# Batch 0 of a linear-attention and MLP kernel: Q cast on its way in the GpSimd queue, narrower weight slices, and a reordered head

## The chip, the core and the metric

The kernel runs on one core of a Trainium2 chip. The metric is the device time of one execution in microseconds (us). Before the change the median of 9 runs is 284.18 us (283.92 to 284.45).

## What is computed

For each of 8 batches and 8 heads (576 rows, 64 columns per head) a K^T V product is formed, Q is multiplied by it, and each row of 64 is divided by its root mean square and scaled by `g_norm`. The heads lie side by side as 4608 rows of 512, and a two-layer MLP with ELU follows.

```python
kv = np.einsum('bhsd,bhse->bhde', k, v)
out = np.einsum('bhsd,bhde->bhse', q, kv)
rms = np.sqrt(np.mean(out * out, axis=-1, keepdims=True) + 1e-06)
x = (out / rms * g_norm).transpose(0, 2, 1, 3).reshape(4608, 512)
h = x @ w_in                                   # 512 -> 2048
g = np.where(h > 0.0, h, np.exp(np.minimum(h, 0.0)) - 1.0)
return g @ w_out                               # 2048 -> 512
```

Inputs and output are fp32; the kernel multiplies in bf16.

## The kernel before, in words

The work is cut into nine groups of 512 rows: group b holds the first 512 rows of batch b, and the ninth holds the last 64 rows of all batches. For each group the attention gives xT (512 features in four blocks of 128, by 512 rows); `mm1` (L446) makes h in eight steps i of two 128-column blocks of w_in each, with four accumulated products a block; `elu` (L474) turns them into gT on ScalarE and VectorE; `mm2` (L507) multiplies pieces of gT by w_out for four row blocks j. The attention of the next group is spread by hand between the products of the current one; the order of the instructions on each engine is the order in which the program is written (`manual_schedule`, L56)[...].

Two kinds of transfers load data. SP's queue (`fetch_q`, L73) moves fp32 as it is. GpSimd's queue casts fp32 to bf16 on the way: `fetch_packed_kv` (L114), `fetch_packed_q` (L96, batches 1 to 7), `load_w_in` (L135), `load_w_out` (L140). [...]

The head, L551 to L755, is batch 0. SP fetches Q of batch 0 in two halves (even and odd heads, 512 KB each). GpSimd issues k and v of batch 0 in eight pieces of two heads, the identity for transposes between them, then w_in in five slices with the edges 0, 512, 768, 1280, 1664 and 2048, then w_out and batch 1. TensorE begins with nine dummy products of zeros (`idle`, L594); more of them stand between the steps, 20 in all. VectorE and ScalarE cast Q to bf16 (`cast_first`, L608), TensorE transposes it in pairs of heads (`turn_first`, L611), and copies put it into qT0.

Batch 0's features come in four columns c (two heads each). For each c: `kv_first` makes K^T V and VectorE copies it to SBUF, `se_first` makes the scores on TensorE, `square_first` squares them on ScalarE, `mean_first` averages them by a product on TensorE, `log_first` and `exp_first` on ScalarE make the inverse root, and `scale_first` on VectorE writes column c of xT. `first(fs, cs)` (L671) then multiplies blocks fs of w_in with columns cs; it makes the first six blocks (24 products) in six banks, and L761 makes the other ten through `mm1` (L465).

From L773 on, the second layer of group 0 is interleaved with the attention of batch 1, in two halves u: `kvu` (K^T V, L357), `seu` (scores), `sq`, `sum`, `inv`, `mulu` (scaling on VectorE), `xu` (transposes and the copy to xT, L404). Group 1's first layer follows at L873. The output of the last group leaves in pieces at L913, the last of them in two halves of 256 columns, each copied by ScalarE (L925) and stored from two queues.

Of the kernel before, what the change touches and what calls it, by code (L numbers as in the profile page):

```python
# [8 lines left out]
FP32 = mybir.dt.float32  # L9
BF16 = mybir.dt.bfloat16  # L10
# [6 lines left out]
def kernel(  # L17
# [20 lines left out]
    J = 4  # L38
# [34 lines left out]
    def fetch_q(b, eng=nc.sync):  # L73

        st = stage_tile("q")[:, 0:2048]
        raw["q", b] = st
        if b < B:
            for s in range(2):
                eng.dma_start(
                    out=st.rearrange("p (s h x) -> p s h x", s=2, h=4)[:, s],  # L80
                    in_=q[b].rearrange("(h s) r d -> s h r d", s=2)[s, :, 0:G, :].rearrange(
                        "h (p j) d -> p h (j d)", j=J
                    ),
                )
# [61 lines left out]
    def copy_on(eng, out_, in_):  # L146
        if eng is nc.scalar:
            nc.scalar.copy(out_, in_)
        else:
            eng.tensor_copy(out=out_, in_=in_)  # L150
# [292 lines left out]

    gT = {}

    def mm1(T, i, cols=(slice(0, 512),), relu=False, home="m1", between=()):  # L446

        if i == 0:
            gT[T] = mlpg.tile([P, FC, G], BF16, name="gT", tag="gT")
        x = xT[T]  # L450
        if home == "m2":
            h_ps = [ps_m2.tile([P, G], FP32, name="h_ps", tag="mm2") for _ in range(2)]
            parts = [(a, a + 1, h_ps[a].rearrange("p (a t) -> p a t", a=1)) for a in range(2)]
        else:
            if home == "at":
                both = at_tile(FP32).rearrange("p (a t) -> p a t", a=2)
            else:
                both = ps_m1.tile([P, 2, G], FP32, name="h_ps", tag="mm1")
            h_ps = [both[:, a, :] for a in range(2)]
            parts = [(0, 2, both)]  # L460
        for cs in cols:
            for a in range(2):
                f = 2 * i + a
                for c in range(KC):
                    nc.tensor.matmul(  # L465
                        h_ps[a][:, cs],
                        lhsT=w_in_sb[:, c, f * P : f * P + P],
                        rhs=x(c, cs),
                        start=(c == 0),
                        stop=(c == KC - 1),  # L470
                    )
        return elu(T, i, parts, relu, between)

    def elu(T, i, parts, relu, between=()):  # L474
# [73 lines left out]

    V, A, Q = nc.vector, nc.scalar, nc.gpsimd

    fetch_q(0)  # L551
    q_raw0 = raw.pop(("q", 0))
    packed_kv(0)
    for c in range(4):
        fetch_packed_kv("k", 0, slice(c, c + 1))
        if c == 2:
            make_identity(nc, ident)
        fetch_packed_kv("v", 0, slice(c, c + 1))
    edges = (0, 512, 768, 1280, 1664, 2048)
    for lo, hi in zip(edges, edges[1:]):  # L560
        load_w_in(slice(lo, hi))
    load_w_out(0, 4)
# [6 lines left out]
    for name in "kv":  # L569
        fetch_packed_kv(name, 1, slice(2, 4))  # L570

    zeros = const.tile([P, 512], BF16, name="zeros")
    nc.vector.memset(zeros, 0.0)  # L573
    means = const.tile([P, P], BF16, name="means")
    nc.vector.memset(means, 0.0)
# [15 lines left out]
    def bank(n):  # L591
        return ps_head.tile([P, G], FP32, name=f"bank{n}", tag=f"bank{n}")

    def idle(ps, n):  # L594
        for _ in range(n):
            nc.tensor.matmul(ps, lhsT=zeros[:, 0:P], rhs=zeros, start=True, stop=True)  # L596

    bank(0), bank(1), bank(2), bank(3)
    kv_ps = ps_head.tile([P, 2, G], FP32, name="kv_ps", tag="kv")
    bank(6), bank(7)  # L600

    idle_ps = bank(1)
    idle(idle_ps, 9)
    q_st = q_raw0.rearrange("p (q h j d) -> p q j h d", q=4, h=2, j=J)
    q_two = attp.tile([P, NPAIR, J, 2, D], BF16, name="q_two", tag="q_two", bufs=1)
    qT0 = attp.tile([P, NPAIR, G], BF16, name="qT", tag="qT")

    def cast_first(pair, eng):  # L608
        copy_on(eng, q_two[:, pair], q_st[:, pair])

    def turn_first(ps, pairs):  # L611
        for r, pair in enumerate(pairs):
            for j in range(J):
                nc.tensor.transpose(ps[:, r, j * P : j * P + P], q_two[:, pair, j], ident)  # L614

    def turned(n):
        return bank(n).bitcast(BF16).rearrange("p (r t) -> p r t", r=2)

    cast_first(0, V)
    cast_first(1, A)  # L620
    qt_ps = turned(3)
    turn_first(qt_ps, (0, 1))
    nc.vector.tensor_copy(out=qT0[:, 0:2], in_=qt_ps)
    idle(idle_ps, 4)
    cast_first(2, V)
    cast_first(3, A)

    kv0 = attp.tile([P, 2, 2, D], BF16, name="kv0", tag="kv0", bufs=1)
    x0 = attp.tile([P, KC, G], BF16, name="xT", tag="xT")
# [22 lines left out]
    def square_first(c):  # L652
        nc.scalar.activation(sq0[c], se0[c], AF.Square)

    def mean_first(c):
        nc.tensor.matmul(mean0[c], lhsT=means, rhs=sq0[c], start=True, stop=True)  # L656
# [22 lines left out]
                    stop=(c == KC - 1),  # L679
                )  # L680

    qt_ps = turned(7)
    turn_first(qt_ps, (2,))
    nc.scalar.copy(qT0[:, 2, :], qt_ps[:, 0, :])
    kv_first(0)
    idle(idle_ps, 1)
    se0[0] = bank(6)
    se_first(0)
    square_first(0)
    qt_ps = turned(0)  # L690
    turn_first(qt_ps, (3,))
    nc.vector.tensor_copy(out=qT0[:, 3, :], in_=qt_ps[:, 0, :])
    idle_ps = bank(3)
    kv_first(1)
    mean0[0] = bank(2)
    mean_first(0)
    log_first(0)
    se0[1] = bank(7)
    se_first(1)
    square_first(1)  # L700
    exp_first(0)
    g_ps = bank(1)
    nc.tensor.matmul(
        g_ps[:, 0:1],
        lhsT=g_row.rearrange("p l d -> p (l d)"),
# [2 lines left out]
        stop=True,  # L708
    )
    nc.vector.tensor_copy(out=g_col, in_=g_ps[:, 0:1])  # L710
    kv_first(2)
    idle(idle_ps, 2)
    se0[2] = bank(1)
    se_first(2)
    square_first(2)
    mean0[1] = bank(0)
    mean_first(1)
    log_first(1)
    exp_first(1)
    idle(idle_ps, 1)  # L720
    kv_first(3)
    scale_first(0)
    idle(idle_ps, 1)
    mean0[2] = bank(2)
    mean_first(2)
    log_first(2)
# [1 line left out]
    se_first(3)  # L728
    square_first(3)
    exp_first(2)  # L730
    idle(bank(0), 2)
    scale_first(1)
    scale_first(2)
    pair = ps_head.tile([P, 2, G], FP32, name="h_ps", tag="kv")
    products = {0: pair[:, 0, :], 1: pair[:, 1, :], 2: bank(6), 3: bank(7), 4: bank(0)}
    first((0, 1, 2, 3), (0,))
    mean0[3] = bank(2)
    mean_first(3)
    log_first(3)
    exp_first(3)  # L740
    scale_first(3)
    products[5] = bank(1)
    first((0, 1, 2, 3), (1, 2))
    first((4,), (0, 1, 2))
    first((0, 1, 2, 3), (3,))
    first((5,), (0, 1, 2))
    first((4, 5), (3,))
    gT[0] = mlpg.tile([P, FC, G], BF16, name="gT", tag="gT")
    single = [
        [(a, a + 1, products[2 * i + a].rearrange("p (a t) -> p a t", a=1)) for a in range(2)]  # L750
# [30 lines left out]
    for j in range(J):  # L781
        mm2_quarter(0, j, 1)
        if j == 1:
            at["kvu0"]()
        if j == 2:
            at["seu0"](scores)
            at["sq0"]()
            at["sum0"]()
    for j in range(J):
        mm2(0, j, 8, 10)  # L790
        if j == 1:
            at["kvu1"]()
            at["inv0"]()
            at["mulu0"]()
    at["seu1"]()
    at["sq1"]()
    at["sum1"]()
    for j in range(J):
        mm2(0, j, 10, 12)
        if j == 1:  # L800
            at["inv1"]()
            at["xu0"](scores[:, 0, :])
# [4 lines left out]
        mm2(0, j, 12, 14)  # L807
    for j in range(J):
        mm2(0, j, 14, FC, hold=j > 1)
        if j == 0:  # L810
            at["xu1"](scores[:, 1, :])
    mm2_out(0, 2)
    mm2_out(0, 3)
# [57 lines left out]
    at, ahead = ahead, attention(3)  # L871
    ahead["qd"]()
    for i in range(8):  # L873
        mm1(1, i, relu=i in (1, 4), home={0: "at", 2: "m2", 5: "m2"}.get(i, "m1"))()
        if i == 3:
            at["kv"]()
    mm2(1, 0, 0, 8)
# [35 lines left out]
    for j, cols in pieces:  # L913
        n = cols.stop - cols.start
        ps = ps_m2.tile([P, DM], FP32, name="o_ps", tag="mm2")[:, 0:n]
        for f in range(FC):
            nc.tensor.matmul(  # L917
                ps,
                lhsT=gT[B][:, f, j * P : j * P + P],
                rhs=w_out_sb[:, f, cols],  # L920
                start=(f == 0),
                stop=(f == FC - 1),
            )
        sb = outp.tile([P, DM], FP32, name="o_last", tag="o_last", bufs=5)[:, 0:n]
        nc.scalar.copy(sb, ps)  # L925
        for l, eng in enumerate((nc.sync, nc.scalar)):
            eng.dma_start(out=rows[l, G:S, j, cols], in_=sb[l * 64 : l * 64 + 64, :])

# [29 lines left out]
```

## Time and profile before

| what | value |
|---|---|
| median of 9 runs | 284.18 us |
| the profiled execution, its own time | 284.04 us |
| its span in the profile | 282.3 us |
| granted TensorE clock | 1.0 |
| TensorE busy | 277.1 us, 98% |
| VectorE / ScalarE / GpSimd busy | 159.3 / 154.5 / 54.7 us |
| GpSimd's transfer queue | 20752 packets, 17.30 MB, 39.9% of 16 engines' span |
| hardware queues of SP and ScalarE | 35348 packets, 17.83 MB, 23.3% |
| GB/s in the first six slices of 7 us | 195, 203, 204, 202, 207, 201 |

The profile covers one execution; times in it count from the start of the span. "Busy" is the time in which an engine executes. The chain of waits is followed back from the last instruction: at each step to what released it, or to the instruction ahead of it on its engine. A line "L674" is line 674 of the kernel above. An issue of a transfer is short; its landing comes later, and "us to landing" is the time between the two.

### The profile page before, as it was taken

How to read it: one execution, taken by the hardware profiler on the slowest of the kernel's cores; microseconds unless marked ns; L12 is line 12 of the kernel's file. 1: busy time of each engine (PE TensorE's matmuls, PEld its weight loads, DVE VectorE, ACT ScalarE, POOL GpSimd, SP SyncE). 2: the span in 40 equal slices, each digit the busy share in tenths (PEclk: the TensorE clock that was granted, in tenths of full speed). 3: DMA queues.
4: the chain of work that ended last, by engine and by line, in shares of the span. 5: the costliest groups of instructions: out<-in, count | busy, mean ns of one | idle time of the engine just before them, and what ended most of it. 6: DMA issues, size and time to landing. Idle time of an engine off the chain costs nothing.

```text
span 282.3 us, 5187 instructions
## 1 busy us (share of the span) xinstructions
PE 277.1 (98%) x2146; PEld 129.7 (46%) x2146; DVE 159.3 (56%) x231; ACT 154.5 (55%) x222; POOL 54.7 (19%) x96
## 2 busy tenths in 40 slices
PE   8999999999999999999999999999999999999994
PEld 3444544445444444444444444444444444444443
DVE  2359353888388546843694469445854585444400
ACT  2779546666487438533863477337823792333311
POOL 7834422251421331006100421012000000000000
PEclk9999999999999999999999999999999999999999
DMA  7999999796992695359835794445333122010122
GB/s 195 203 204 202 207 201 187 197 178 128 190 191 56 157 174 138 74 149 132 188 75 149 94 221 80 116 110 148 58 96 70 78 55 93 0 77 0 74 77 74
DMA packets 56523, 35.99 MB, mean 127 GB/s; under 512 B 32820, under 2 KB 54068, under 8 KB 56500
## 3 DMA queue, kind: packets, MB, share of 16 engines
q0 software_dynamic: 20752, 17.30, 39.9%
q1 hardware_dynamic: 35348, 17.83, 23.3%
q10 hardware_dynamic: 400, 0.52, 0.6%
q8 instruction: 17, 0.28, 0.4%
q14 instruction: 6, 0.05, 0.0%
HBM read 36.70 MB, written 9.44 MB: 163 GB/s over the span
## 4 chain that ended last, share of the span: by engine, by line
PE 98%; DVE 0%; ACT 0%; issue 0%
PE h_ps L465 42%; PE o_ps L512 39%; PE o_ps L917 5%; PE bank L596 2%; PE at L174 2%; PE bank L674 1%; PE at L465 1%; PE at L201 1%; PE h_ps L674 1%; PE bank L614 1%; PE bank L644 1%; PE se_ps L201 1%; PE kv_ps L174 0%; PE at L185 0%; PE se_ps L413 0%; PE bank L656 0%
## 5 line engine op out<-in xcount | busy, mean ns | idle before, releaser
L465 PE MATMUL h_ps<-xT,w_in_sb 128*128 128x512 bf16 x536 | 125.7, 379 | 0.0
L512 PE MATMUL o_ps<-w_out_sb,gT 128*128 128x512 bf16 x512 | 120.5, 379 | 0.0
L477 ACT ACTIVATE elu_e<-h_ps 128x1024 bf16<-128x1024 f32 (+1 forms) x71 | 70.0, 995 | 80.0 <-PE h_ps L465 77.8
L465 PEld LDWEIGHTS <-w_in_sb 128*128 128x128 bf16 x552 | 52.5, 98 | 63.2 <-DVE xT L333 1.7
L512 PEld LDWEIGHTS <-gT 128*128 128x128 bf16 x512 | 49.4, 98 | 58.4 <-DVE gT L496 0.3
L488 DVE TENSOR_SCALAR elu_e<-elu_e 128x1024 bf16<-128x1024 bf16 (+1 forms) x75 | 32.5, 433 | 73.2 <-ACT elu_e L477 73.2
L496 DVE TENSOR_TENSOR gT<-elu_e,h_ps 128x1024 bf16<-128x1024 bf16 (+1 forms) x51 | 60.1, 1179 | 5.7 <-DVE elu_e L488 0.5
L525 ACT COPY o_sb<-o_ps 128x512 f32<-128x512 f32 x32 | 18.6, 586 | 15.4 <-PE o_ps L512 15.4
L218 DVE TENSOR_REDUCE ss<-sq 128x16 f32<-128x1024 bf16 x16 | 19.4, 1218 | 10.8 <-ACT sq L213 10.1
L483 ACT ACTIVATE elu_h<-h_ps 128x1024 bf16<-128x1024 f32 (+1 forms) x20 | 19.5, 990 | 0.0
L150 POOL COPY q_bf<-q_pk 128x512 bf16<-128x512 bf16 x24 | 14.6, 636 | 20.3 <-DMA q_pk<-in_q_dram 20.3
L496 DVE TENSOR_TENSOR gT<-elu_e,elu_h 128x1024 bf16<-128x1024 bf16 x20 | 13.8, 692 | 2.8 <-ACT elu_h L483 1.5
L917 PE MATMUL o_ps<-w_out_sb,gT 128*128 128x512 bf16 (+1 forms) x80 | 14.1, 337 | 0.0
L125 POOL COPY gate<-qT 1x1 bf16<-1x1 bf16 x6 | 1.1, 182 | 63.1 <-DMA qT<-q_bf 63.1
L104 POOL DMA_DIRECT2D q_pk<-in_q_dram x14 | 10.6, 764 | 2.8 <-issue 1.1
L229 DVE TENSOR_TENSOR xs<-at,ss 128x512 bf16<-128x512 f32 x16 | 10.2, 683 | 1.2 <-ACT ss L225 1.2
L917 PEld LDWEIGHTS <-gT 128*128 128x128 bf16 x80 | 7.7, 98 | 6.4 <-DVE gT L496 0.4
L213 ACT ACTIVATE sq<-at 128x1024 bf16<-128x1024 f32 x9 | 9.4, 1043 | 1.6 <-PE at L201 1.0
L118 POOL DMA_DIRECT2D k_pk<-in_k_dram x12 | 8.3, 691 | 4.5 <-DMA w_in_sb<-in_moe_w_in_dram 3.0
L118 POOL DMA_DIRECT2D v_pk<-in_v_dram x12 | 8.3, 688 | 4.4 <-DMA w_out_sb<-in_moe_w_out_dram 1.8
L596 PE MATMUL bank<-zeros 128*128 128x512 bf16 x20 | 7.8, 518 | 1.2 <-DVE zeros L573 1.2
L925 ACT COPY o_last<-o_ps 128x512 f32<-128x512 f32 (+1 forms) x5 | 2.5, 501 | 10.8 <-PE o_ps L917 10.8
(79 smaller groups left out, 139.5 us busy)
## 6 DMA issues: line engine op xcount, KB each, us to landing
out_dram<-o_sb SPq DMA_DIRECT2D x16, 512.0 KB, 3.1
q_pk<-in_q_dram POOLq DMA_DIRECT2D x14, 256.0 KB, 4.8
k_pk<-in_k_dram POOLq DMA_DIRECT2D x6, 576.0 KB, 7.6
v_pk<-in_v_dram POOLq DMA_DIRECT2D x6, 576.0 KB, 10.6
st_q<-in_q_dram SPq DMA_DIRECT2D x2, 512.0 KB, 5.6
w_in_sb<-in_moe_w_in_dram POOLq DMA_DIRECT2D x2, 512.0 KB, 8.9
w_out_sb<-in_moe_w_out_dram POOLq DMA_DIRECT2D x2, 512.0 KB, 15.6
w_out_sb<-in_moe_w_out_dram POOLq DMA_DIRECT2D x4, 256.0 KB, 11.8
```

The lines of the kernel that those rows point to most:

```text
L118: nc.gpsimd.dma_start(out=raw[name, b].rearrange("p h j d -> p h (j d)")[:, hs], in_=in_[:, hs])
L150: eng.tensor_copy(out=out_, in_=in_)
L218: nc.vector.reduce_sum(out=ss, in_=sq.rearrange("p c (h e) -> p (c h) e", h=H), axis=AX.X)
L465: nc.tensor.matmul(h_ps[a][:, cs], lhsT=w_in_sb[:, c, f * P : f * P + P], rhs=x(c, cs), start=(c == 0), stop=(c == KC - 1),)
L477: nc.scalar.activation(e[:, lo:hi, :], ps, AF.Exp)
L483: nc.scalar.activation(h[:, lo:hi, :], ps, AF.Relu)
L488: nc.vector.tensor_scalar(out=e[:, lo:hi, :], in0=e[:, lo:hi, :], scalar1=1.0, scalar2=1.0, op0=ALU.min, op1=ALU.subtract,)
L496: nc.vector.tensor_tensor(out=gT[T][:, 2 * i + lo : 2 * i + hi, :], in0=e[:, lo:hi, :], in1=h, op=ALU.add if relu else ALU.max,)
L512: nc.tensor.matmul(o_ps[T, j], lhsT=gT[T][:, f, j * P : j * P + P], rhs=w_out_sb[:, f, :], start=(f == 0), stop=(f == FC - 1),)
L525: nc.scalar.copy(o_sb[T][:, j % 2, :], o_ps.pop((T, j)))
L596: nc.tensor.matmul(ps, lhsT=zeros[:, 0:P], rhs=zeros, start=True, stop=True)
L917: nc.tensor.matmul(ps, lhsT=gT[B][:, f, j * P : j * P + P], rhs=w_out_sb[:, f, cols], start=(f == 0), stop=(f == FC - 1),)
```

## The change

In batch 0's head, Q no longer comes through SP. It is fetched by the GpSimd queue, cast on the way, in two halves of four heads (256 KB each in bf16): heads 0 to 3 ahead of all other transfers, heads 4 to 7 behind the second v piece. The casts on VectorE and ScalarE go. Each half is transposed by 16 transposes of 64-column heads (`turn_heads`, eight of 128 columns before) and copied by one VectorE instruction. The first 1280 columns of w_in come in five slices of 256 (before: 512, 256, 512). The steps of the four columns are reordered: the product for `g_norm` comes earlier, heads 4 to 7 are transposed behind the second K^T V, the second mean comes ahead of the third scores. The dummies are cut from 20 to five, two of them in fp32, for which the tile of zeros is doubled. `first` makes blocks 0 and 1 for columns 0 and 1 ahead of blocks 2 and 3.

In batch 1, the second K^T V stands behind all four pieces (8, 10) of the second layer and not behind the second of them; its scores, squares and sums stand behind the first piece (10, 12), and its transposes behind the third piece (14, FC). The first step of group 1's first layer goes through both blocks column by column (`by_c`). In the last store the ScalarE copy of 256 columns becomes two of 128, one on VectorE.

Of the waits in TensorE's list: the first transpose waits for heads 0 to 3, the transposes of heads 4 to 7 stand ahead of the first mean product, blocks 2 and 3 of `first` wait for the second slice of w_in, block 4 for the third.

```diff
-    def mm1(T, i, cols=(slice(0, 512),), relu=False, home="m1", between=()):
+    def mm1(T, i, cols=(slice(0, 512),), relu=False, home="m1", between=(), by_c=False):
...
-            for a in range(2):
+            steps = [(a, c) for a in range(2) for c in range(KC)]
+            if by_c:
+                steps.sort(key=lambda step: step[1])
+            for a, c in steps:
                 f = 2 * i + a
...
-    fetch_q(0)
-    q_raw0 = raw.pop(("q", 0))
+    q_first = packed.tile([P, H, J, D], BF16, name="q_pk", tag="q")
+
+    def fetch_heads(eng, out_, lo):
+        eng.dma_start(
+            out=out_.rearrange("p (h x) -> p h x", h=4),
+            in_=q[0, lo : lo + 4, 0:G, :].rearrange("h (p j) d -> p h (j d)", j=J),
+        )
+
+    fetch_heads(nc.gpsimd, q_first[:, 0:4].rearrange("p h j d -> p (h j d)"), 0)
     packed_kv(0)
     for c in range(4):
         fetch_packed_kv("k", 0, slice(c, c + 1))
-        if c == 2:
+        fetch_packed_kv("v", 0, slice(c, c + 1))
+        if c == 1:
             make_identity(nc, ident)
-        fetch_packed_kv("v", 0, slice(c, c + 1))
-    edges = (0, 512, 768, 1280, 1664, 2048)
+            fetch_heads(nc.gpsimd, q_first[:, 4:8].rearrange("p h j d -> p (h j d)"), 4)
+    edges = (0, 256, 512, 768, 1024, 1280, 1664, 2048)
...
-    zeros = const.tile([P, 512], BF16, name="zeros")
+    zeros = const.tile([P, 1024], BF16, name="zeros")
...
-    def idle(ps, n):
+    def idle(ps, n, dtype=BF16):
+        z = zeros.bitcast(dtype)
         for _ in range(n):
-            nc.tensor.matmul(ps, lhsT=zeros[:, 0:P], rhs=zeros, start=True, stop=True)
+            nc.tensor.matmul(ps, lhsT=z[:, 0:P], rhs=z[:, 0:512], start=True, stop=True)
...
-    idle(idle_ps, 9)
+    idle(idle_ps, 2, FP32)
+    idle(idle_ps, 1)
...
+    def turn_heads(u):
+        qt_ps = turned(3)
+        for s in range(2):
+            for j in range(J):
+                for l in range(2):
+                    nc.tensor.transpose(
+                        qt_ps[l * 64 : l * 64 + 64, s, j * P : j * P + P],
+                        q_first[:, 4 * u + 2 * l + s, j, :],
+                        ident,
+                    )
+        nc.vector.tensor_copy(out=qT_u[:, u], in_=qt_ps)
+
+    turn_heads(0)
...
     kv_first(0)
...
+    idle(idle_ps, 1)
+    se0[0] = bank(6)
+    se_first(0)
+    square_first(0)
+    kv_first(1)
+    turn_heads(1)
+    mean0[0] = bank(2)
+    mean_first(0)
+    log_first(0)
+    se0[1] = bank(7)
+    se_first(1)
+    square_first(1)
+    exp_first(0)
     kv_first(2)
-    idle(idle_ps, 2)
+    mean0[1] = bank(0)
+    mean_first(1)
+    log_first(1)
+    idle(idle_ps, 1)
     se0[2] = bank(1)
     se_first(2)
     square_first(2)
...
-    first((0, 1, 2, 3), (0,))
+    first((0, 1), (0, 1))
     mean0[3] = bank(2)
     mean_first(3)
...
-    first((0, 1, 2, 3), (1, 2))
+    first((2, 3), (0, 1))
+    first((0, 1, 2, 3), (2,))
     first((4,), (0, 1, 2))
-    first((0, 1, 2, 3), (3,))
-    first((5,), (0, 1, 2))
-    first((4, 5), (3,))
+    first((0, 1, 2, 3, 4), (3,))
+    first((5,), range(KC))
...
     for j in range(J):
         mm2(0, j, 8, 10)
-        if j == 1:
-            at["kvu1"]()
...
+    at["kvu1"]()
     for j in range(J):
         mm2(0, j, 10, 12)
+        if j == 0:
+            at["seu1"]()
+            at["sq1"]()
+            at["sum1"]()
...
         mm2(0, j, 14, FC, hold=j > 1)
-        if j == 0:
+        if j == 2:
             at["xu1"](scores[:, 1, :])
...
-        nc.scalar.copy(sb, ps)
+        if cols.stop == DM and n < DM:
+            nc.scalar.copy(sb[:, 0 : n // 2], ps[:, 0 : n // 2])
+            nc.vector.tensor_copy(out=sb[:, n // 2 : n], in_=ps[:, n // 2 : n])
+        else:
+            nc.scalar.copy(sb, ps)
```

More of the change, by code (lines that the diff above doesn't have):

```diff
@@ L461, in mm1 @@
         for cs in cols:
-            for a in range(2):
+            steps = [(a, c) for a in range(2) for c in range(KC)]
+            if by_c:
+                steps.sort(key=lambda step: step[1])
+            for a, c in steps:
                 f = 2 * i + a
[L464 to L471, printed above, removed]
+                nc.tensor.matmul(
+                    h_ps[a][:, cs],
+                    lhsT=w_in_sb[:, c, f * P : f * P + P],
+                    rhs=x(c, cs),
+                    start=(c == 0),
+                    stop=(c == KC - 1),
+                )
         return elu(T, i, parts, relu, between)
@@ L602 @@
     idle_ps = bank(1)
-    idle(idle_ps, 9)
-    q_st = q_raw0.rearrange("p (q h j d) -> p q j h d", q=4, h=2, j=J)
-    q_two = attp.tile([P, NPAIR, J, 2, D], BF16, name="q_two", tag="q_two", bufs=1)
+    idle(idle_ps, 2, FP32)
+    idle(idle_ps, 1)
     qT0 = attp.tile([P, NPAIR, G], BF16, name="qT", tag="qT")
[L608 to L614, printed above, removed]
     def turned(n):
         return bank(n).bitcast(BF16).rearrange("p (r t) -> p r t", r=2)
[L619 to L626, printed above, removed]
+    qT_u = qT0.rearrange("p (s u) t -> p u s t", u=2)
+    def turn_heads(u):
[7 more added lines that the diff above has]
+                        ident,
+                    )
+        nc.vector.tensor_copy(out=qT_u[:, u], in_=qt_ps)
+    turn_heads(0)
     kv0 = attp.tile([P, 2, 2, D], BF16, name="kv0", tag="kv0", bufs=1)
@@ L680, in first @@
                 )
-    qt_ps = turned(7)
-    turn_first(qt_ps, (2,))
-    nc.scalar.copy(qT0[:, 2, :], qt_ps[:, 0, :])
     kv_first(0)
[L686 to L702, printed above, removed]
+    g_ps = bank(2)
     nc.tensor.matmul(
@@ L715 @@
     square_first(2)
-    mean0[1] = bank(0)
-    mean_first(1)
-    log_first(1)
     exp_first(1)
-    idle(idle_ps, 1)
+    scale_first(0)
     kv_first(3)
-    scale_first(0)
-    idle(idle_ps, 1)
     mean0[2] = bank(2)
@@ L730 @@
     exp_first(2)
-    idle(bank(0), 2)
     scale_first(1)
@@ L734 @@
     pair = ps_head.tile([P, 2, G], FP32, name="h_ps", tag="kv")
-    products = {0: pair[:, 0, :], 1: pair[:, 1, :], 2: bank(6), 3: bank(7), 4: bank(0)}
-    first((0, 1, 2, 3), (0,))
+    products = {0: pair[:, 0, :], 1: pair[:, 1, :], 2: bank(6), 3: bank(0), 4: bank(7)}
+    first((0, 1), (0, 1))
     mean0[3] = bank(2)
@@ L788 @@
             at["sum0"]()
+    at["inv0"]()
+    at["mulu0"]()
     for j in range(J):
         mm2(0, j, 8, 10)
-        if j == 1:
-            at["kvu1"]()
[L793 to L797, printed above, removed]
+    at["kvu1"]()
     for j in range(J):
         mm2(0, j, 10, 12)
+        if j == 0:
+            at["seu1"]()
+            at["sq1"]()
+            at["sum1"]()
         if j == 1:
@@ L873 @@
     for i in range(8):
-        mm1(1, i, relu=i in (1, 4), home={0: "at", 2: "m2", 5: "m2"}.get(i, "m1"))()
+        mm1(1, i, relu=i in (1, 4), home={0: "at", 2: "m2", 5: "m2"}.get(i, "m1"), by_c=i == 0)()
         if i == 3:
```

## The prediction

> **What bounds the kernel now.** I read the page first (busy shares), then the chain of work that ended last in order of time, then the timeline and the transfers of the first 20 us.
>
> ```profile
> PE 277.1 (98%) x2146; PEld 129.7 (46%) x2146; DVE 159.3 (56%) x231; ACT 154.5 (55%) x222; POOL 54.7 (19%) x96
> ```
>
> TensorE is busy in all but 5.2 us of the 282.3 us span. 1.2 of these lie ahead of its first instruction and 3.9 behind its last (the last copy and store). So the end is "when TensorE starts real work, plus that work, plus the tail". The chain, whose columns are start, length, engine and line, shows which of its work is padding:
>
> ```profile
> 1.22 4.02 PE bank L596 x9
> 5.24 0.85 PE bank L614 x8
> ...
> 13.89 0.54 PE bank L596 x2
> 14.43 0.49 PE h_ps L674 x2
> ...
> 18.48 1.51 PE bank L674 x7
> 20.00 5.18 PE h_ps L465 x24
> ```
>
> L596 are dummy products. From 14.43 on all is needed: the 24 head products of L674 and one mean product end at 20.00, and from there no wait is left in the chain. What started the products is in the timeline:
>
> ```profile
> 14.32 0.55 PEld L674 LDWEIGHTS <-w_in_sb 128*128 128x128 bf16 x4 [0.38 <-DMA w_in_sb<-in_moe_w_in_dram]
> 15.58 0.75 DVE L665 SCALAR_TENSOR_TENSOR xT<-bank,g_col,r 128x512 bf16<-128x512 f32 x1 [0.78 <-ACT r L662]
> 17.00 0.75 DVE L665 SCALAR_TENSOR_TENSOR xT<-bank,g_col,r 128x512 bf16<-128x512 f32 x1 [0.67 <-ACT r L662]
> ```
>
> The first weight slice ended the wait (issued 7.05, 7.2 us to landing); the xT columns arrive just in time behind it. So the head is bound by transfers. For the first 20 us, in 40 slices of 0.5 us, and for the first k issue (1.24) and five later Q issues of 256 KB that found the GpSimd queue empty (each answer for a stretch with that issue alone):
>
> ```profile
> GB/s 0 0 0 8 31 211 385 383 381 384 273 246 222 196 212 198 203 207 203 196 210 203 198 207 211 205 207 192 227 186 198 203 207 213 205 194 204 208 201 198
> k_pk<-in_k_dram POOLq DMA_DIRECT2D x1, 144.0 KB, 5.5
> ```
> ```profile
> q_pk<-in_q_dram POOLq DMA_DIRECT2D x1, 256.0 KB, 4.1
> q_pk<-in_q_dram POOLq DMA_DIRECT2D x1, 256.0 KB, 4.2
> q_pk<-in_q_dram POOLq DMA_DIRECT2D x1, 256.0 KB, 4.3
> q_pk<-in_q_dram POOLq DMA_DIRECT2D x1, 256.0 KB, 4.4
> ```
>
> Q of batch 0 moves at 384 GB/s on SP's queue as fp32 (1 MB) up to 5 us; from then on the GpSimd queue, which casts, moves 200 GB/s of bf16. Its first packet is at 4.95, 3.7 us after the issue.
>
> [...] 1.46 to 1.58 us in the five later starts, 3.7 at the head. [...] beside a 16 KB instruction packet at 14.3 one engine falls 1.0 us behind (15 parts of the second w_in slice by 15.62, the last at 16.70), and stays so in all later slices. [...] dummies start 0.427 us apart up to 6.3 and 0.22 from 6.74 on.
>
> **The change part by part.**
> *Queue.* SP loses 1 MB; the GpSimd queue gains 2 x 256 KB, heads 0-3 ahead of everything, heads 4-7 behind the second v slice. Moving them costs about the same (1 MB at 384 is 2.7 us; 512 KB in 512-byte packets at 1.37 us each, the distance of the two Q landings in the later starts, is 2.74). What matters is when heads 0-3 land; I call that q0. Lower: 4.35 (packets at 2.7 as in the later starts, full rate at once: 1.24 + 1.46 + 1.37 + 0.25 spread). Upper: 6.5 (first packet at 4.95 as now). I take 1.24 + 4.3 = 5.5, the middle of five starts of the same transfer.
> *Slices behind it.* Eight k/v slices land 0.71 apart (7 steps from 6.77 to 11.74): 5.68. Heads 4-7 and the first two w_in slices of 256 columns: 3 x 1.37 = 4.11. I add 0.2 for switching between Q and k (in the later starts k took 0.2 to 0.7 more than 576 KB at 205), and the 1.0 lag, because the instruction packet came just as the w_in wait opened, at PE row 240, which the changed order has at the same place. The second slice lands at q0 + 11.0 = 16.5; now the first 512 columns have landed at 14.28.
> *Products.* Four products and the mean need only the first slice (about 14.1) and the xT columns 0 and 1; 25 less these is 20 products x 0.216 = 4.32 behind the second slice: end at q0 + 15.3 = 20.8, against 20.0. Break-even: q0 = 4.7.
> *Head chain.* The two casts before transposes go (0.43 DVE, 0.62 ACT), as do 17 of 20 bf16 dummies; of five products left two are fp32. All lay under transfers: nothing. The 16 transposes of heads 4-7 stand ahead of the first mean product, so behind their wait are that product, the log on ACT and all 11 ACT steps behind it. Heads 4-7 land at 5.5 + 0.2 + 2.84 + 1.37 = 9.9, transposes 0.5 (32 took 1.01 at L185), mean 0.22: log at 10.7 against 10.06. The chain's last exp ends at 17.6 (now 16.96), its xT column at 18.3, 9 products later 20.3: hidden behind 20.8.
> *zeros* doubles: memset 0.27 to 0.55, dummies from 1.5: hidden. g's product earlier: hidden.
> *Batch 1.* The queue is about 1.4 later by the end of w_in (5.5 + 0.2 + 5.68 + 1.37 + 5 x 1.37 + 2 x 1.95 + 1.0 = 24.5, now 23.06), TensorE 0.8 later: waits lose 0.6 of slack. First k/v half: landed 33.63, used 34.93: 0.7 stays. Second: 37.81 against 38.48, and moved behind four more products (0.86): 0.9 stays. w_out columns 10-12: 39.06 against 40.20, scores moved behind them (0.34): 0.2 stays. Nothing is paid; if that cover goes, 0.2 to 0.5. The transposes moved to j == 2 come at 45.4 in today's times, their xs at 44.9; x at 46.7, while by_c gives the first group of batch 1 four products (to 47.3) that don't need it: nothing.
> *Tail.* The last copy, 0.37 on ACT, is halved over two engines: 0.0 to 0.2 gained, I take 0.1.
> Sum: +0.8 - 0.1 = +0.7 on the profiled execution's own 284.04 (span 282.3 and 1.7 around it) is 284.7; the median lies 0.14 above that execution: 284.9.
>
> **Rivals.**
> 1. *Late start* (q0 6.5): the 3.7 us at the head belong to the queue's first use and not to SP's traffic. For: packets start at once at full share at 4.95, with none of the slow ramp of the later starts. Against: SP held the engines at 384 GB/s just until then. End at 21.8: +1.7, 285.9.
> 2. *Early start*, the other side: SP's 1 MB was all that held the GpSimd queue back; with it gone heads 0-3 land at 4.35. Price: q0 + 15.3 = 19.65, or with no switching loss 19.45: -0.35 to -0.55, the tail 0.1; without the instruction lag on the second slice, another 0.3 until the ACT chain binds. 283.3 to 283.7. It decides below q0 = 4.6. Against: all five later starts took 4.1 to 4.4 in an otherwise nearly quiet DMA.
> 3. *Nothing to see*: q0 about 5.0 (in the later starts landing came 1.9 us after the third issue ended, which is at 3.1 here), or the instruction packet elsewhere (-1.0 from the second slice, then the ACT chain holds 20.3). End at 20.0 to 20.3: 284.1 to 284.5.
> 4. *Cold clock*: [...] nothing fills 5.4 to 7. If the clock then rises a window later, scores, means and transposes double along the chain: about +1.5, 286.4.
>
> **How the numbers follow.** Main case 0.37 (284.6 to 285.3), late start 0.20, cold clock 0.05, nothing to see 0.22, early start 0.16. A measurement of this kernel can tell about 0.2% (0.57 us) from no change: faster is the early start, 0.16; within 0.2% are rival 3 and a small part of the main case, 0.25; slower 0.59. The range leaves out half of the early start and the worst of the slow ones: 283.5 to 286.0; the main case alone has 284.6 to 285.3.
>
> **What would show it.** In the profile after: the first Q wait of TensorE ends near 5.5; the second w_in slice near 16.5 ends a TensorE wait of about 1 us inside L683; L467 starts near 20.8 and no wait follows. Wrong if Q lands before 4.7, if that wait is absent, or if dummies and scores keep 0.427 spacing past 7.

## The result and the profile after

| what | before | after |
|---|---|---|
| median | 284.18 us | 288.71 us (10 runs, 286.65 to 290.03) |
| after against before | | 1.0159, interval 1.0146 to 1.0173 |
| the profiled execution, its span | 284.04, 282.3 | 288.75, 287.0 |
| heads 0 to 3 of Q landed | (SP, in halves by pairs) | 5.96 |
| heads 4 to 7 of Q landed | | 10.76 |
| first logarithm on ScalarE | 10.06 | 12.44 |
| first product with w_in, L683 | 14.32 | 17.14 |
| product 25, the first of L467 | 19.83 | 24.46 |
| last product ends | 278.44 | 283.01 |

The change makes the kernel 1.6% slower, and the prediction (284.9) was wrong by 3.8 us. The loss is in the head: 4.63 of the 4.7 us that the span grew are there at product 25 (24.46 less 19.83), and behind it TensorE has no gap. TensorE's busy share does not show it (97% against 98%), since a product at half clock counts as busy too (four take 1.71 us on the chain below, where five take 1.08 at full clock). From the page of after:

```profile
PE 279.8 (97%) x2149; PEld 131.8 (46%) x2149; DVE 159.5 (56%) x230; ACT 152.7 (53%) x219; POOL 58.0 (20%) x100
```

The chain of waits of after for the first 26 us (start, length, engine and line):

```profile
4.81 5.95 DMA q_pk<-in_q_dram
...
10.80 1.06 PE bank L628 x16
11.87 0.55 PE bank L665
...
12.44 0.69 ACT r L668
...
17.20 1.82 PE h_ps L683 x4
19.02 0.43 PE bank L665
19.45 1.71 PE bank L683 x4
21.16 0.44 PE h_ps L683 x2
21.60 1.08 PE bank L683 x5
22.68 0.43 PE h_ps L683 x2
23.11 1.51 PE bank L683 x7
```

Two things are to be seen. The chain now enters through the landing of heads 4 to 7 (L628 are their transposes, L665 is the mean, L668 the logarithm). And four products take 1.82 and 1.71 where later five take 1.08: 0.43 to 0.46 each against 0.216. Up to 21 us TensorE runs at half clock. The timeline of TensorE in after tells the same from the start on (start, length, line, operation, count, and in brackets the idle time ahead with what ended it):

```profile
1.49 4.21 PE L607 MATMUL bank<-zeros 128*128 128x512 f32 x5 [1.49 <-DVE zeros L583]
6.01 1.07 PE L628 MATMUL bank<-ident,q_pk 128*64 128x128 bf16 x16 [0.31 <-DMA q_pk<-in_q_dram]
7.84 0.69 PE L174 MATMUL kv_ps<-v_pk,k_pk 64*64 64x64 bf16 x18 [0.77 <-DMA v_pk<-in_v_dram]
10.80 1.06 PE L628 MATMUL bank<-ident,q_pk 128*64 128x128 bf16 x16 [0.18 <-DMA q_pk<-in_q_dram]
17.14 1.89 PE L683 MATMUL h_ps<-xT,w_in_sb 128*128 128x512 bf16 x4
```

The two fp32 dummies are four records, 0.853 us apart behind the first, and with the bf16 one they end at 5.69. Then come a wait, transposes, another wait: nothing dense any more. In the trace's record of the granted clock, before goes to full at 6.74 and stays; in after the first entry, to full, is at 21.06. (The view by stretches prints 1.00 ahead of a first entry, so there the spacing has to be read.) The mean clock shown for the other nine runs of after is 0.976 to 0.987: 0.982 means 0.018 x 287 / 0.5 = 10.3 us at half clock. Half clock ahead of a first entry is not in such a mean (the profiled run is shown with 1.0), so these nine had a recorded stretch at half, most likely as in experiment 3 below, where the clock rose, fell and rose again and the mean is 0.976; no trace of them was kept. Their times follow it: 286.65 at 0.987, 288.07 to 288.71 at 0.981 and 0.982, 289.51 to 290.03 at 0.976.

The transfers of after, GB/s in 40 slices of the first 20 us:

```profile
GB/s 0 0 0 0 1 12 51 147 140 200 195 155 141 166 189 199 178 193 189 215 194 198 201 196 201 192 190 184 199 198 193 196 222 183 192 193 199 195 198 207
```

Packets of the GpSimd queue now begin at 2.84 and not at 4.95, but from 3 to 6 us they move only 148 GB/s on average. The tail, from the timeline of after:

```profile
283.05 0.27 ACT L926 COPY o_last<-o_ps 128x128 f32<-128x128 f32 x1 [1.37 <-PE o_ps L917]
283.35 0.29 DVE L927 COPY o_last<-o_ps 128x128 f32<-128x128 f32 x1 [11.40 <-ACT o_last L926]
```

VectorE's half of the last copy waits for ScalarE's half: 0.59 from first start to last end, where the undivided copy takes 0.37.

### The profile page after: what moved, and what is told of

Read it like the earlier page. It is cut to its first block, busy times and chain, and to the rows that moved or that the text cites. A ratio compares the mean times of both kernels' runs of the same rounds, so it can differ in the third digit from the quotient of the medians.

```text
span 287.0 us, 5189 instructions
## 1 busy us (share of the span) xinstructions
PE 279.8 (97%) x2149; PEld 131.8 (46%) x2149; DVE 159.5 (56%) x230; ACT 152.7 (53%) x219; POOL 58.0 (20%) x100
## 4 chain that ended last, share of the span: by engine, by line
PE 94%; DMA 2%; POOL 1%; ACT 1%; issue 0%; DVE 0%; POOLq 0%
PE h_ps L467 41%; PE o_ps L514 39%; PE o_ps L917 5%; DMA q_pk<-in_q_dram 2%; PE at L174 2%; PE bank L683 1%; PE at L467 1%; PE at L201 1%; PE h_ps L683 1%; PE bank L665 1%; PE se_ps L201 0%; PE bank L653 0%; ACT sq L662 0%; POOL k_pk L118 0%; PE bank L628 0%
## 5 line engine op out<-in xcount | busy, mean ns | idle before, releaser
L467 PE MATMUL h_ps<-xT,w_in_sb 128*128 128x512 bf16 x536 | 125.7, 379 | 0.0
L467 PEld LDWEIGHTS <-w_in_sb 128*128 128x128 bf16 x552 | 52.5, 98 | 63.2 <-DVE xT L333 1.7
L218 DVE TENSOR_REDUCE ss<-sq 128x16 f32<-128x1024 bf16 x16 | 19.4, 1218 | 11.0 <-ACT sq L213 10.3
L174 PEld LDWEIGHTS <-k_pk 64*64 64x64 bf16 x576 | 7.8, 112 | 4.8 <-issue 4.7
L224 ACT ACTIVATE ss<-ss,eps_col 128x16 f32<-128x16 f32 x16 | 5.1, 317 | 4.1 <-DVE ss L218 4.1
```

The costliest lines, as they stand in the source:

```text
L174: nc.tensor.matmul(kv_ps[l * 64 : l * 64 + 64, s, u * 64 : u * 64 + 64], lhsT=bf["k", T][rows, j, 2 * u + l, :], rhs=bf["v", T][rows, j, 2 ...
L218: nc.vector.reduce_sum(out=ss, in_=sq.rearrange("p c (h e) -> p (c h) e", h=H), axis=AX.X)
L467: nc.tensor.matmul(h_ps[a][:, cs], lhsT=w_in_sb[:, c, f * P : f * P + P], rhs=x(c, cs), start=(c == 0), stop=(c == KC - 1),)
```

## The experiments

The theory after the result: the removed dummies had kept the clock up, and without them the clock stays or falls back to half (the gap form). A rival inside it: the clock is late because the dummies are fp32 (the fp32 form). A rival beside it: the later landing of Q and the new order of the head hold the chain, whatever the clock does. The kernel before, run beside each of them, had medians of 283.97 to 284.08.

### 1. The kernel before with fp32 dummies

```diff
-    idle(idle_ps, 9)
+    idle(idle_ps, 2, FP32)
+    idle(idle_ps, 1)
```

> The kernel before with one edit: the first nine bf16 dummies become two fp32 and one bf16 (as in the changed kernel); the four dummies at 5.9 us and all other work stay. Clock theory, fp32 form (fp32 products do not count towards the rise of the clock): the clock rises one or two windows later than 6.7 us, products stand 0.427 us apart until then, 285.5 to 287.5 us. Clock theory, gap form (what is missing are dummies between 5.4 and 8 us): they are still here, so 6.7 us and 284.2. Queue theory (the later landing of Q and w_in made the time): nothing of the queue is changed, 284.2.

Measured: 284.46 (283.97 to 285.59), 1.0018 [1.0004, 1.0032]. The clock rose at 5.92 and stayed, product 25 started at 19.91, 0.08 later than in before. The fp32 form, which asked for 285.5 or more, falls. Four of the 12 runs took 285.12 to 285.59; the trace kept is of one at 284.19 and doesn't tell why.

### 2. The kernel before with its later dummies thinned out

Nine of the eleven dummies behind the first nine are gone, nothing else.

```diff
-    idle(idle_ps, 4)
...
-    idle(idle_ps, 2)
+    idle(idle_ps, 1)
...
-    idle(idle_ps, 1)
...
-    idle(idle_ps, 1)
...
-    idle(bank(0), 2)
```

> The kernel before with nine of the eleven later dummies taken out; the first nine bf16 ones and one ahead of the first and of the third scores stay. Clock theory, gap form: the clock rises late, 285.5 to 287.5 us. Fp32 form: the nine are bf16, the clock rises at 6.7 us as now, 284.1 to 284.3. Queue theory: 284.2.

Measured: 287.86 (287.01 to 288.88), 1.0139 [1.0107, 1.0170]. The view by stretches of this kernel (stretch and its length, busy time and count for PE, PEld, DVE, ACT and POOL, then the granted clock, DMA share, GB/s):

```profile
5.00:7.00 2.00, 1.00 (x9) 0.76 (x8) 0.97 (x3) 0.47 (x2) 1.20 (x3) 1.00 1.19 233
7.00:9.00 2.00, 1.74 (x29) 1.04 (x29) 0.44 (x2) 1.05 (x3) 1.86 (x3) 1.00 1.21 203
9.00:11.00 2.00, 2.00 (x26) 0.99 (x23) 0.72 (x2) 1.18 (x3) 2.00 (x4) 0.54 1.21 203
...
17.00:19.00 2.00, 2.00 (x6) 0.76 (x5) 0.35 (x1) 1.15 (x2) 0.70 (x1) 0.50 1.29 204
19.00:21.00 2.00, 2.00 (x10) 0.84 (x9) 0.75 (x1) 0.16 (x1) 0.71 (x1) 0.90 1.31 203
```

The clock is full after the nine first dummies (from 5.76), falls to half at 9.17 and is full again at 19.41. The 3.41 us ahead of the fall hold one long wait (1.22), where four dummies had stood. From the timeline of the same kernel:

```profile
7.21 0.40 PE L614 MATMUL bank<-ident,q_two 128*128 128x128 bf16 x4 [1.22 <-DVE q_two L150]
```

Only dummies were taken out. The slices of w_in land 0.1 to 0.5 later than in before, but no product waits for them, and yet product 25 starts at 22.80 in place of 19.83. Dummies that the prediction held for covered by transfers were worth 3.8 us. The gap form is shown, in the kernel before. (The two slowest of the four runs are shown with a mean clock of 1.0, like the profiled run of after: that figure alone doesn't tell that the clock was held.)

### 3. The kernel after with bf16 dummies ahead

```diff
-    idle(idle_ps, 2, FP32)
+    idle(idle_ps, 8)
```

> The changed kernel with its two fp32 dummies replaced by eight bf16 ones of the same length in total (3.4 us); all else stays. Fp32 form of the clock theory: the clock rises by 7 to 10 us, the first layer starts near 21.3 us, 285.2 to 286 us. Gap form: the clock stays at half until about 21 us, 288.7. Queue theory: 288 to 288.7.

Measured: 288.96 (288.42 to 289.78), 1.0168 [1.0143, 1.0192]. The clock rose at 5.73, fell at 9.15, rose at 22.80. As in 2, dense dummies at the start are not enough: behind the gaps at 5.5 (0.52) and 6.7 (1.14) the clock goes down again, and the one at 10.0 (1.18) lies behind the fall. The time is that of the gap form, but the course is not: it had the clock at half throughout.

### 4. The kernel after with some gaps filled

```diff
-    idle(idle_ps, 2, FP32)
-    idle(idle_ps, 1)
+    idle(idle_ps, 10)
...
     turn_heads(0)
+    idle(idle_ps, 2)
...
+    idle(idle_ps, 1)
     turn_heads(1)
```

> The changed kernel with ten bf16 dummies first, two more behind the transposes of heads 0 to 3 and one more ahead of those of heads 4 to 7, all in places where TensorE waits for a transfer. Clock theory, both forms: the clock rises near 7 us, products stand 0.216 us apart, the first layer's second part starts near 21.3 us; of the 4.5 us that the change costs 1.2 to 1.5 stay (the queue's share): 285.2 to 285.7 us. Queue theory: 288 to 288.7.

Measured: 287.16 (285.87 to 288.55), 1.0103 [1.0055, 1.0151]: between the two forecasts. It falls into two groups: two runs whose mean clock is 0.997 and 1.0 took 285.87 and 286.06, two with 0.987 and 0.988 took 288.27 and 288.55. In the profile, one of the latter, the clock fell at 13.57, behind a wait of 1.40 us for heads 4 to 7. The same kernel with the clock held and with it lost for a time is thus 2.4 us apart.

### 5. The kernel after with the clock held

Ten dummies ahead, and 4, 1, 6, 3, 3 and 2 at the later places.

```diff
     turn_heads(0)
+    idle(idle_ps, 4)
...
     square_first(0)
     kv_first(1)
+    idle(idle_ps, 6)
     turn_heads(1)
...
     exp_first(0)
+    idle(idle_ps, 3)
```

> The changed kernel with bf16 dummies in every place where TensorE waits in the head (10, 4, 1, 6, 3, 1, 3 and 2 of them)[...]. If the clock's falling back is most of the change's cost: it rises near 6 us and stays, products stand 0.216 us apart, and what remains over the kernel before is the queue's share: 285.4 to 286.0 us, runs within 0.5 us of each other. If the clock is only a small part and the later Q is the main one: 287 us or more even with a held clock.

Measured: 286.71 (286.65 to 286.91), 1.0098 [1.0083, 1.0113]: between the two forecasts. In the profile the clock rose at 6.45 and stayed, and the four runs lie within 0.3 of each other. Product 25 starts at 22.15, still 2.3 later than in before. From the chain of this kernel:

```profile
10.01 1.40 PE bank L607 x6
11.41 0.57 PE bank L627 x16
11.98 0.32 PE bank L665
12.30 0.33 PE bank L653 x2
12.63 0.75 PE bank L607 x3
```

The transposes (L627) take 0.57 and not 1.06, but the dummies (L607) now lie on the chain: the landing of heads 4 to 7 at 11.16 was over when the six ended. Each one too many costs its 0.216.

### 6, 7 and 8. Three attempts at what is left

In 6, heads 0 to 3 came by SP in fp32 and were cast on VectorE and ScalarE, heads 4 to 7 stayed in the GpSimd queue. In 7, all of Q came by SP, and the GpSimd transfer of heads 4 to 7 went. In 8 (kernel 5 otherwise), the transposes of heads 4 to 7 stood behind the first mean and the second scores. All three had dummies at much the same places as kernel 5, in 6 and 7 fewer of them.

```diff
-    fetch_heads(nc.gpsimd, q_first[:, 0:4].rearrange("p h j d -> p (h j d)"), 0)
+    q_st = stage_tile("q")
+    sp_heads(q_st[:, 0:1024], 0)
+    sp_heads(q_st[:, 1024:2048], 4)
...
-            fetch_heads(nc.gpsimd, q_first[:, 4:8].rearrange("p h j d -> p (h j d)"), 4)
```

The diff is that of 7; 6 has neither its last added nor its last removed line.

> As x5, but heads 0 to 3 come by SP as fp32 (512 KB) and are cast on VectorE and ScalarE; heads 4 to 7 stay in the GpSimd queue. If the queue's first 4.5 us are what is left of the cost: heads 0 to 3 ready by 5.1 instead of 6.0, all GpSimd transfers about 1 us earlier than in x5, head end near 19 to 19.7: 283.0 to 283.8 us. If the order of the head (transposes of heads 4 to 7 ahead of the first mean, narrow slices) is what is left: 285 us or more.

Measured: 286.07 (285.42 to 286.16), 1.0066 [1.0050, 1.0083]. The first forecast was missed; the time is in the range of the second, but the chain names a landing and not the order. Heads 0 to 3 landed at 4.46, but heads 4 to 7 only at 11.02, because one of the 16 DMA engines brought its part 1.3 us behind the others (9.73); the first mean came at 11.64. The wait for the second half of Q sets the chain, not that for the first.

> As x5, but all of Q comes by SP as fp32 in two transfers of four heads and is cast on VectorE and ScalarE, as in the kernel before; slices, order and tail are those of the changed kernel. Queue theory of the rest: the second w_in slice lands near 14.5 to 15.5, head end 19 to 20: 283.0 to 284.0 us. If slices and order are what is left: 285 us or more.

Measured: 287.36 (285.93 to 288.97), 1.0121 [1.0073, 1.0168]. Inconclusive: TensorE waited 1.49 us for v at 6.69, and the clock fell at 8.93. The two runs with a mean clock of 0.999 and 1.0 took 286.39 and 285.93.

> As x5, but the transposes of heads 4 to 7 stand behind the first mean product and the second scores, so that ScalarE's chain no longer waits for heads 4 to 7 (10.8 us). If that wait sets the head's end (through the 11 ScalarE steps behind it): log at about 10.2 instead of 11.8, head end 0.5 to 1 us earlier than x5. If the second w_in slice sets it (at q0 + 15.3): as x5 within 0.2 us.

Measured: 286.88 (286.34 to 288.53), 1.0112 [1.0081, 1.0144], as 5. The clock held. The first logarithm came at 10.62 (in 5 at 12.34), but product 25 at 22.32. The dummies that fill the moved place are on the chain in its stead, so this run doesn't tell what the place of the transposes is worth.

### 9 and 10. Clock held with fewer dummies, and Q on SP beside it

9 is kernel 5 with 10, 4, 4, 1, 2 and 1 dummies. 10 is kernel 7 with 8, 6, 2, 1, 3 and 1; six of them fill the wait for v.

> The changed kernel with bf16 dummies only where they should end ahead of the awaited transfer (10, 4, 0, 4, 1, 1, 2 and 1), nine fewer in the middle than a full fill puts on the chain. With the clock held, the head ends at 21.2 to 21.8 us (x5: 22.4), 285.5 to 286.0 us: what the queue and the order cost with a full clock. If the dummies of x5 were not on the chain: 286.6 as x5. If the fill is too thin the clock falls back: 287 us or more, runs spread over more than 1 us.

Measured: 286.43 (285.79 to 287.48), 1.0083 [1.0068, 1.0098]; product 25 at 21.51, as expected, the time 0.4 above its forecast. Against after the held clock is worth 288.71 - 286.43 = 2.3 us, net of what its dummies cost on the chain. At product 25 it is 2.95; some is given back at 41.45, where TensorE waits 0.32 for a slice of w_out.

> The changed kernel with all of Q on SP in fp32 and cast on VectorE and ScalarE, and dummies set for these arrivals (8, 6, 2, 0, 1, 1, 3 and 1), so that the clock holds where x7 lost it. If the GpSimd transfer of Q is what is left of the cost with a full clock: the first mean no longer waits for heads 4 to 7, head end near 20, 283.8 to 284.5 us. If the order and the slices are what is left: 285.5 us or more.

Measured: 285.46 (285.27 to 286.00), 1.0052 [1.0040, 1.0064]; clock full from 6.22, product 25 at 20.74. So Q in the GpSimd queue costs 286.43 - 285.46 = 1.0 us, with dummies set for each of the two; how much of it is the dummies' was not run apart. The time lies at the edge of the forecast by which order and slices are left. From the chain of 10:

```profile
9.86 0.40 PE kv_ps L174 x18
10.26 0.57 PE bank L642 x16
10.83 0.34 PE bank L682
```

Q has long landed (6.85), and still the first mean (L682) comes at 10.83, behind the 16 transposes (L642).

### 11 to 14. The other parts, in the kernel before

11 takes over the moves in batch 1, `by_c` and the split of the last copy; 12 the narrow slices of w_in and the new order of the 24 products; 13 the split of the last copy alone; 14 is 11 without it. Their diffs are the parts of the change's diff.

> The kernel before with only the late parts of the change: batch 1's second K^T V, its scores and its transposes later, the first step of group 1 column by column, and the last copy halved over ScalarE and VectorE. The head is untouched. By the prediction batch 1's moves cost and gain nothing and the tail gains 0.1. By the profile of the changed kernel the two halves run one after the other (0.27 and 0.29 us), so the tail loses 0.1 to 0.2: 284.1 to 284.3 us. Over 284.5 us: the moves cost something that no wait showed.

Measured: 284.54 (284.36 to 284.93), 1.0018 [1.0011, 1.0025]: more than expected. Product 25 at 19.82 and the last product's end at 278.37 are unmoved.

> The kernel before with only the narrow w_in slices and the new order of the first 24 products; Q, dummies and head chain as before. The first slice lands at about 13.1, but xT's first column is there at 14.1 and the last dummies end at 14.4: the products start where they did, and the second slice is there by 15.4: 283.8 to 284.3 us. If narrow slices by themselves cost transfers or waits: 284.7 us or more.

Measured: 284.05 (283.93 to 284.80), 1.0003 [0.9995, 1.0011]. The first slices landed at 13.07 and 14.40; the products start at 14.22 as before.

> The kernel before with the last store's copy split over ScalarE and VectorE, nothing else. If the tail is the whole of the +0.5 that tail and batch-1 moves cost together: 284.4 to 284.6, with TensorE's last end unmoved at 278.4 and the second half of the copy starting where the first ends. If only the later end of the copy counts (0.56 in place of 0.37): 284.2 to 284.3.

Measured: 284.61 (284.41 to 284.98), 1.0021 [1.0013, 1.0029]: the split copy is the whole of it, +0.57. From the end of the last product to the end of the span it is 4.29 us (282.8 less 278.51) where it was 3.86. The stores are issued 0.22 later behind that product (0.66 in place of 0.44), and the rest is their landing, some 0.2 longer. From the timeline of 13:

```profile
278.55 0.27 ACT L926 COPY o_last<-o_ps 128x128 f32<-128x128 f32 x1 [1.37 <-PE o_ps L917]
278.85 0.29 DVE L927 COPY o_last<-o_ps 128x128 f32<-128x128 f32 x1 [11.40 <-ACT o_last L926]
```

> The kernel before with the moves in batch 1 and the column-by-column step of group 1, the tail as it was. If these cost nothing, as the prediction had it: 283.9 to 284.2. If they take part in the +0.5: 284.3 to 284.5, with a gap of TensorE between 38 and 50 us.

Measured: 283.99 (283.82 to 284.06), 0.9997 [0.9989, 1.0006]: the moves in batch 1 cost nothing.

### 15. Q on SP, clock held, transposes early

```diff
     cast_heads(q_st[:, 1024:2048], 4)
-    idle(idle_ps, 6)
+    idle(idle_ps, 5)
+    turn_heads(1)
...
-    idle(idle_ps, 2)
+    idle(idle_ps, 1)
     kv_first(1)
-    turn_heads(1)
```

> The kernel after with all Q on SP and the clock held by bf16 dummies (the version at 285.46), and the transposes of heads 4 to 7 directly behind those of heads 0 to 3, five dummies between them, ahead of the wait on the first v piece; one dummy less ahead of the second K^T V. If the place of these transposes is most of what is left of the loss: first mean at about 10.2 (before 10.06, there 10.8), end of the 24 products at 20.0 to 20.4, 284.7 to 285.1. If the transfers or the dummies of the later head hold it: no change, 285.3 to 285.6. The clock has to be full from about 6.5 on for either to be read.

Measured: 285.11 (284.94 to 285.61), 1.0038 [1.0026, 1.0051]; product 25 at 20.49, 0.25 ahead of 10. The transposes of heads 4 to 7 also have a bank of their own here. Just outside the weak end of what the order theory expected: in this profile the mean came at 10.56, behind a copy of qT (0.69) that the scores wait for.

### 16. The last copy in two tiles

```diff
-        nc.scalar.copy(sb, ps)
+        if cols.stop == DM and n < DM:
+            for a, copy in enumerate((nc.scalar.copy, nc.vector.tensor_copy)):
+                sb = outp.tile([P, DM], FP32, name="o_last", tag="o_last", bufs=6)[:, 0 : n // 2]
+                copy(sb, ps[:, a * (n // 2) : (a + 1) * (n // 2)])
...
```

> The kernel before with the last copy split over ScalarE and VectorE into two tiles of their own, each stored in two transfers of 32 KB. If the one tile that both halves write is what puts them one after the other (0.56 in place of 0.37): they run side by side, 0.29, and the time is 284.0 to 284.2, the 0.1 that is won against the two more stores. If they still follow each other[...]: 284.5 to 284.7.

Measured: 285.37 (285.27 to 285.54), 1.0046 [1.0032, 1.0059]: above both forecasts. From its timeline:

```profile
278.38 0.27 ACT L927 COPY o_last<-o_ps 128x128 f32<-128x128 f32 x1 [1.37 <-PE o_ps L917]
278.67 1.11 SPq L930 DMA_DIRECT2D out_dram<-o_last  x2
278.68 1.39 ACTq L930 DMA_DIRECT2D out_dram<-o_last  x2
278.68 0.29 DVE L927 COPY o_last<-o_ps 128x128 f32<-128x128 f32 x1 [11.40 <-ACT o_last L927]
```

With tiles of their own the halves still follow each other: VectorE's starts at 278.68, 0.03 behind the end of ScalarE's, and what ended VectorE's wait is ScalarE's copy. So the tile they write is not the cause. What they still share is the tile that they read, `o_ps`; that this is the cause was not shown, as a split over two tiles to read was not run. The 0.8 beyond run 13 (285.37 less 284.61) are put down to the four stores, two on each queue; this was not tested apart.

### 17. Kernel 15 with the undivided copy

> The version at 285.11 (Q on SP, clock held, early transposes) with the last copy by ScalarE alone, as before. If the terms add up: 285.11 less the 0.57 that the split costs in the kernel before, 284.4 to 284.7, which is the time before plus its later end of the 24 products (0.66 in the profiles). If the split costs less behind this head: 284.9 to 285.1.

Measured: 284.52 (284.20 to 284.85), 1.0015 [1.0008, 1.0021]; product 25 at 20.33. The split costs 285.11 - 284.52 = 0.59 here, 0.57 in the kernel before. No version was found that is faster than before.

## Why the prediction was wrong

The loss, taken apart step by step (medians; each row is the one above it with one more part undone, and down to 15 with its dummies set anew):

| version | us | the step |
|---|---|---|
| after | 288.71 | |
| 9: clock held | 286.43 | 2.3 clock |
| 10: and Q on SP | 285.46 | 1.0 transfer of Q |
| 15: and transposes early | 285.11 | 0.35 order (the intervals of 10 and 15 overlap) |
| 17: and the copy undivided | 284.52 | 0.6 tail |
| before | 284.08 | 0.44 left |

*The step that failed* is "17 of 20 bf16 dummies; of five products left two are fp32. All lay under transfers: nothing". That they lay under transfers is right, but they did a second thing: they kept the clock up through the waits. With them it is full from 6.74 on in before; with nine of them taken out and nothing else (2) it is half from 9.17 to 19.41, which cost 3.8 us; in after it is 2.3, most of the 3.8 by which the forecast was short. The form of the two that are left matters little (1: 0.2%, 3: nothing). The mechanism stood among the rivals as the cold clock, with the words "the clock then rises a window later", a price of 1.5 and a chance of 0.05, and its sign came, spacing of 0.427 past 7. The price was the author's estimate for one window. In the profiled run of after the clock is half until 21.06, so transposes, means, scores and the first eight products run at half clock. That the waits behind the dummies (they end at 5.69; from 7 to 9 TensorE is busy for 1.23 of 2 us) are what holds it there is argued from 2, not shown in after itself. The reading error came before that: the spacing of 0.427 and 0.22 was looked at as a matter of when the clock first rises, and no one asked what holds it from then on. In 2, 3, 4 and 7 it fell behind 3.41 us in which TensorE had been idle for 1.27 to 1.49 (last section).

*The queue.* Heads 0 to 3: 5.5 predicted, 5.96 measured. The late start is wrong in its cause: without SP's 1 MB packets began at 2.84 and not at 4.95. The runs have three sizes of SP's traffic: with 1 MB of Q on SP the first packet came at 4.5 to 5.0, with 512 KB (6) at 3.46, with none at 2.83 to 2.87. But the early start is wrong too: at 148 GB/s the transfer wasn't over at 4.35, and its 16 parts landed from 4.75 to 5.96, a spread of 1.2 where the working had 0.25. The second slice of w_in: 16.5 predicted, 16.38 measured, in part by luck. Of the 1.0 that the working had for one engine falling behind beside the instruction packet nothing came there: the packet ran at 16.17, and in the third slice the last part is 0.64 behind the one ahead (18.35, 17.71). Instead the parts of the second were spread from 15.32 to 16.38. And nobody waits for it, as the products begin at 17.14; the wait that was to show the step right is absent, and this was named as what would make it wrong.

*Heads 4 to 7.* "Heads 4-7 land at ... 9.9" and "log at 10.7": they landed at 10.76, and the logarithm came at 12.44. The difference of 1.74 is 0.86 of the landing and, at half clock, 0.56 of the transposes (1.06 in place of 0.5) and 0.33 of the mean (0.55 in place of 0.22). This, and not the second slice, became the bound: also with the clock held (9) the transfer of Q costs 1.0. That it is near the 0.8 of the forecast is luck, as it comes through another wait.

*The tail.* "Halved over two engines: 0.0 to 0.2 gained": it costs 0.57 by the medians of 13, because the halves run one after the other. (Behind the last product the spans go on for 3.99 to 4.53 us with the split copy, in after, 11, 13 and 15, and for 3.82 to 3.88 with the undivided one, in before, 12, 14 and 17.)

*Right* were: the slices and the products' order cost nothing by themselves (12), and the batch-1 moves cost nothing (14).

*Open* are the 0.44 us between 17 and before. Three dummies ahead of the third mean are on 17's chain with 0.75 us, and product 25 is 0.50 late; that they are the rest is argued, not shown. That the casts went from VectorE and ScalarE is no gain that a run shows: with them back, 10 is faster than 9.

## What to carry to other kernels

A filler product has two prices. On the chain it costs its 0.216 us. Off the chain its price is the clock: nine fewer cost 3.8 us in 2, where the products behind them stood 0.43 us apart in place of 0.216. So ask of each removed filler how long TensorE then stands idle; in 2 it was 1.22 us in one wait where four had stood. And before counting on a copy halved over two engines, look in the timeline whether the halves run side by side: here the second started 0.03 us behind the end of the first, into one tile (13) and into two (16).

## What the hardware showed beyond that

*When the clock falls.* In run 2 the entries of the clock record (5.76, 9.17 and 19.41) are 3.41 and 10.24 us apart, once and three times the same. The idle time of TensorE in 3.41 us counted from the rise (in the second window of 4, from the end of the first), by the trace:

```
run                window            idle us   clock behind it
12                 4.08 to  7.50     1.08      full
16                 4.75 to  8.16     0.81      full
4, first window    6.74 to 10.16     0.81      full
9                  6.61 to 10.03     0.53      full
before             6.74 to 10.15     0.15      full
2                  5.76 to  9.17     1.27      half
4, second window  10.16 to 13.57     1.33      half
3                  5.73 to  9.15     1.44      half
7                  5.51 to  8.93     1.49      half
```

These nine are what was measured, with modelled ends of products. The longest single wait is 0.84 in the window of 12 (full) and 0.87 in the second of 4 (half). Whether the sum or the longest wait counts was not tested.

*When it rises again* is less clear. In 2 the window from 16.00 without idle time, all products and a mean, was followed by the rise; the one from 12.58 with only 0.16 idle, made of K^T V products of 64x64, scores of 64 rows and means, was not. In before and after, the 3.41 us ahead of the first rise (6.74 and 21.06) have no idle time; in after, the four windows ahead of that, with 0.22 to 0.64 idle, brought none. Yet in 12 the window from 0.67 with 0.55 idle, the rest dummies of 512 columns, was followed by the rise at 4.08. What in a window brings the rise, no run isolates.

*One late DMA engine.* In 6 a single engine, 1.3 us behind the other 15 (9.73), made heads 4 to 7 land at 11.02, and their transposes started at 11.07.
